# Attention's software pipeline one step shorter: probabilities turned 3 and values applied 4 steps behind the scores, the last logits in another order, expert-search columns 12 to 18 counted in one accumulation

## The chip, the cores and the metric

The kernel runs on one core of one Trainium2 chip. Its engines are TensorE (matmuls, PE in the profile, with its weight loads as PEld), VectorE (DVE), ScalarE (ACT), GpSimd (POOL) and SyncE (SP, which here only starts transfers). Each engine takes its own instructions in the order in which they were written and waits at an instruction until its inputs and its output buffer are free. The metric is device time in microseconds (us), the median of the runs.

## The reference

Three blocks follow one another: a sparse attention, a mixture of experts in which every token goes to one of 8 experts with room for 288 each, and a second mixture over 4 experts in which every token goes to all.

```python
scores = scale * np.matmul(q, k.transpose(0, 1, 3, 2))          # 4 batches, 8 heads, 576 x 64
mask_local = (rel >= 0) & (rel < stride)                        # heads 0..3, stride 32
mask_strided = (rel >= 0) & (pos[None, :] % stride == pos[:, None] % stride)   # heads 4..7
attn = softmax(where(masks, scores, -1e9)); attn_out = attn @ v
logits = x @ w_gate                                             # 2304 tokens, 8 experts
order = np.argsort(-logits.flatten())                           # best pairs first
for idx in order:
    tok, e = (int(idx) // E, int(idx) % E)
    if assigned[tok] >= 0 or counts[e] >= cap:
        continue
    assigned[tok] = e; counts[e] += 1
out[mask] = relu(x[mask] @ w1[e]) @ w2[e]                       # per expert
y = sum over 4 experts of p[:, e] * (relu(out @ v1[e]) @ v2[e])
```

## The kernel before

`front` computes the attention and the logits. The masks leave blocks only, so the work is cut into N = 40 units: for each of the 4 batches, 5 units of strided heads (`kind` 1, blocks of 126 or 108 rows) and 5 of local heads (128 queries by 96 keys, the last of them half as large). A loop over steps t writes out a software pipeline by hand. In step t stand, in this order of the program: dummy matmuls in the first 8 steps (`keep_busy`), then `tr_p(t-4)`, `norm(t-2)`, the queued pieces of token work (`late2`, `late`), up to two `piece`s (transposes of q and k of the next batch) around `exps(t-1)`, `logits(t-10)`, `av(t-5)` and `scores(t)`.

For one unit n: `scores` is TensorE's product of q and k into the PSUM tile `s`, which has one buffer, and VectorE's masked reduction into `sm` and `mx`. `exps` is ScalarE's exponential into `pr`, with row sums `su`. `norm` is VectorE's reciprocal `r` and a multiplication of `pr` by it on GpSimd. `tr_p` turns `pr` round on TensorE into the PSUM tile `pt`, which has one buffer, and ScalarE copies it out to `pT`. `av` multiplies by the values into the PSUM tile `av`, one buffer, and copies go into `hold`: by VectorE for strided units, by ScalarE for local ones. GpSimd also starts six transfers of v (`load_v`, line 78) in step 2, 12 and 22, ahead of that step's `norm`, and in step 28 one of `side` (line 403).

The copies of `piece` for q, and those of the logits, alternate between ScalarE and VectorE by a counter that all calls of `copy` raise:

```python
flip[0] += 1
ch = side_of[eng]
if ch == "a" or (ch == "f" and flip[0] % 2):
```

After the last scores (steps N = 40 to 45) the pipeline drains: `keep_busy(2)` puts two dummy matmuls of 512 columns into each of steps 41 to 44, the logits of units N-3 and N-1 (local groups 2 and 4 of the last batch) are made in steps 43 to 45, and `tokens` turns them to the layout `L`, tokens by 18 columns by 8 experts.

The search for the first expert begins with a count over these 18 columns: for each column `best` marks each token's best expert and `reach` compares its logit with 127 thresholds, and `first_count` multiplies the two on TensorE. Columns 0 to 11 are counted batch by batch during the attention, columns 12 to 13 in the drain, each group in its own PSUM accumulation that VectorE adds to `cnt`. Columns 14 to 17 follow in `search`, in `experts`, and are added to `cnt` there. `experts` begins with that search, in which TensorE and VectorE take turns, and with the transposes of the remaining attention rows (`deferred`, line 295 and 284); then rows are gathered by expert and the two mixtures run, which is the long rest of the kernel.

Of the kernel before, what the change touches and what calls it, by code (L numbers as in the profile page):

```python
# [18 lines left out]
FT = mybir.dt.float32  # L19
# [18 lines left out]
def front(tc, ident, hot, q, k, v, wg, dp, xd, L, ready, hold, deferred):  # L38
# [3 lines left out]
    with ExitStack() as st:  # L42
# [173 lines left out]
        def norm(n):  # L216
            T = U[n]
            rows, keys, na = shape(n)
            e = T["p"][:rows, :2 * na, :keys]
            r = wk.tile([128, 4], FT, name="r")[:rows, :2 * na]  # L220
            nc.vector.tensor_scalar(r, T["su"][:rows, :2 * na], 1e-9, None, op0=OP.add)
            nc.vector.reciprocal(r, r)
            nc.gpsimd.tensor_tensor(e, e, r[:, :, None].to_broadcast([rows, 2 * na, keys]), OP.mult)

        def tr_p(n):
            T = U[n]
# [89 lines left out]
                rows_q.pop(0)[1](*here, lambda o, i: copy(o, i, eng=eng))  # L316

        def logits(n):
            b, kind, g = units[n]
            if kind or g not in (2, 4):  # L320
                return
            i0, m = (0, 128) if g == 2 else (128, 160)
            p = LP[n] = ps.tile([128, 512], FT, name="xr", bufs=2)
            for h in range(4):
                nc.tensor.matmul(p[32 * h:32 * h + 32, :m], wgs[:, h], XTS[b].rearrange("p h j r -> p h (j r)")[:, h, i0:i0 + m], start=True, stop=False)
            if n < N - 1:
                logits_local(n)

        LP = {}

        def logits_local(n):
            b, kind, g = units[n]
            i0, m = (0, 128) if g == 2 else (128, 160)
            p = LP[n]
            for par in range(2):
                for hp in range(2):
                    c = 32 * (2 * par + hp)
                    nc.tensor.matmul(p[c:c + 32, :m], wgl[:, hp, 8 - 8 * par:40 - 8 * par], XTL[b][:, hp, 2 * i0 + par:2 * i0 + 2 * m:2],
                                     start=False, stop=True)
            lg = wk.tile([128, 160], FT, name="lg")  # L340
            copy(lg[:, :m], p[:, :m], eng="l")
            late.append(lambda: tokens(b, g // 4, lg))

        late, late2 = [], []
# [1 line left out]
        def tokens(b, q, lg):  # L346
            p = ps.tile([128, 512], FT, name="xr", bufs=2)
            nc.tensor.matmul(p[:, :16], lg[:, :128], four[:, :16], start=True, stop=True)
            copy(L[:, 4 * b + 2 * q:4 * b + 2 * q + 2, :], p[:, :16].rearrange("p (a e) -> p a e", a=2), eng="k")
            if q:  # L350
                w = slice(32 * b, 32 * b + 32)
                p = ps.tile([128, 512], FT, name="xr", bufs=2)
                nc.tensor.matmul(p[w, :16], lg[:, 128:], four[:, :16], start=True, stop=True)
                copy(L[w, 16:], p[w, :16].rearrange("p (a e) -> p a e", a=2), eng="k")
            if q == b // 3:
                return
            c0, c1 = (4 * b, 4 * b + 4) if q else (12, 14)
            late2.append(lambda: ready[0](c0, c1))
            late2.append(None)
            G = wk.tile([128, 4, 128], BF, name="g0")  # L360
            late2.append(lambda: ready[1](G, c0, c1))
            late2.append(None)
            late2.append(None)

            def count():
                p = ps.tile([128, 512], FT, name="xr", bufs=2)
                ready[2](G, p, c0, c1)
            late2.append(count)
# [13 lines left out]
        for t in range(N + 14):  # L382
            t_now[0] = t
            if t < N and t % 10 == 2 and units[t][0] + 1 < B:
                if units[t][0] + 2 < B:
                    load_qk(units[t][0] + 2, "s")
                load_v(units[t][0] + 1)
                if units[t][0] + 2 < B:
                    load_qk(units[t][0] + 2, "l")
                nxt = [(units[t][0] + 1, i) for i in ORDER]  # L390

            if t < N and t % 10 == 6 and units[t][0] + 1 < B:
                load_vl(units[t][0] + 1)
            if t == 28:
                side = cst.tile([128, 18, 8], FT, name="side")
                nc.gpsimd.memset(side, 0.0)
                nc.gpsimd.iota(side.bitcast(I32)[:, :, 4], pattern=[[1, 18]], base=0, channel_multiplier=18)
                rs = cst.tile([128, 18], FT, name="rs")
                nc.vector.tensor_reduce(rs, pr, AX.X, OP.add)
                nc.vector.tensor_scalar(rs, rs, 1e-9, None, op0=OP.add)  # L400
                nc.vector.reciprocal(rs, rs)
                nc.vector.tensor_tensor(side[:, :, :4], pr, rs[:, :, None].to_broadcast([128, 18, 4]), OP.mult)
                nc.gpsimd.dma_start(dap(xd, 512, [18 * XW, 128], [XW, 18], [1, 8]), side)
            if t % 10 == 6:
                todo += nxt
                nxt = []

            def at(d, f):
                if 0 <= t - d < N:
                    f(t - d)  # L410

            def pre():
                if todo and t:
                    piece(*todo.pop(0))

            def keep_busy(n):
                p = ps.tile([128, 512], FT, name="xr", bufs=2)
                for i in range(n):
                    nc.tensor.matmul(p, hot[:, :128], hot, start=True, stop=True)

            if BUSY[0] <= t < BUSY[1]:
                keep_busy(BUSY[2] + 2 * (t < 2))
            at(4, tr_p)
            if N < t < N + 5:
                keep_busy(2)
            at(2, norm)
            while late2:
                x = late2.pop(0)
                if x is None:
                    break  # L430
                x()
            while late:
                late.pop(0)()
            rows("o")
            pre()
            at(1, exps)
            rows("s")
            pre()
            if t < N:
                at(10, logits)  # L440
            elif t == N + 3:
                logits(N - 3)
            elif t == N + 4:
                logits(N - 1)
            elif t == N + 5:
                logits_local(N - 1)
            at(5, av)
            if t < N:
                scores(t)
        for x in late2 + late:  # L450
# [15 lines left out]
def route_consts(nc, cst):  # L466
# [56 lines left out]
                  cst.tile([128, NC, 8], FT, name="eq0")]  # L523
    nc.vector.memset(K["first"][2], 0.0)
    K["cnt"] = cst.tile([8, 128], FT, name="cnt0")
    K["sat"] = cst.tile([128, 1], BF, name="sat")
    nc.vector.memset(K["sat"], 0.0)
    return K
# [20 lines left out]
def first_best(nc, K, L, c0, c1):  # L549
    for _ in best(nc, K, L, K["first"], c0, c1):  # L550
        pass
# [6 lines left out]
def whole(oh, c):  # L558
    return oh[:, c:c + 4, :].rearrange("p a e -> p (a e)")


def first_count(nc, K, G, p, c0, c1):
    for c in range(c0, c1):
        nc.tensor.matmul(p[:, :127], whole(K["first"][2], c), G[:, c - c0, 1:128], start=c == c0, stop=c == c1 - 1)
    if c0 == 0:
        nc.vector.tensor_copy(K["cnt"][:, :127], p[:8, :127])
    elif c0 < 14:
        nc.vector.tensor_tensor(K["cnt"][:, :127], p[:8, :127], K["cnt"][:, :127], OP.add)


def search(nc, K, wk, ps, L, g, S, out):
# [5 lines left out]
    if g < 7:  # L577
# [5 lines left out]
        for r, (nb, sh) in enumerate(rounds):  # L583
# [6 lines left out]
            if g == 0 and r == 0:  # L590
                G = wk.tile([128, 4, 128], BF, name="G")
                first_best(nc, K, L, 14, 18)
                first_reach(nc, K, G, 14, 18)
                yield "2"
                first_count(nc, K, G, p, 14, 18)
                yield "p"
                nc.vector.tensor_tensor(junk[:, 1:], p[:8, :127], K["cnt"][:, :127], OP.add)
# [765 lines left out]
def attention_moe_moe(ctx, tc, q, k, v, wg, w1, w2, dp, v1, v2, out):  # L1363
    nc = tc.nc
    ctx.enter_context(tc.manual_schedule())
    cp = ctx.enter_context(tc.tile_pool(name="c", bufs=1))
    dr = ctx.enter_context(tc.tile_pool(name="dr", bufs=1, space=bass.MemoryType.DRAM))
    ident = cp.tile([128, 128], FT, name="ident")
    hot = cp.tile([128, 512], BF, name="hot")
    nc.vector.memset(hot, 1.0)  # L1370
    make_identity(nc, ident)
    L = cp.tile([128, 18, 8], FT, name="L")
    xd = dr.tile([2304, XW], FT, name="xd")
    side = dr.tile([2304, 8], FT, name="side")
    K = route_consts(nc, cp)
    yp = ctx.enter_context(tc.tile_pool(name="yp", bufs=1))
    ready = (lambda *a: first_best(nc, K, L, *a), lambda *a: first_reach(nc, K, *a), lambda *a: first_count(nc, K, *a))
    hold = lambda: yp.tile([128, 2304], FT, name="hold", bufs=3)
    deferred = []
    front(tc, ident, hot, q, k, v, wg, dp, xd, L, ready, hold, deferred)  # L1380
    experts(tc, ident, hot, K, L, xd, side, w1, w2, v1, v2, out, hold, deferred)
# [26 lines left out]
```

## Time and profile before

| | us |
|---|---|
| median of 3 runs | 1177.46 (1176.71 to 1178.22) |
| profiled execution, its own time | 1176.97 |
| its span, first to last instruction | 1175.3 |
| TensorE busy over the span | 1146.8 (98%) |
| exponentials of the last unit start | 107.26 |
| first instruction of the search on columns 14 to 17 | 117.49 |
| first matmul of the first expert | 146.09 |

Times in rows are counted from the span's start. The kernel has three stretches in time: the attention to about 108 us, the drain, the search and the gather to 146 us, and the experts from there to the end. Only the first two hold instructions that the change touches. "Step t" below is the step of the loop in which `scores(t)` is made, and "unit n" the unit.

### The profile page before, as it was taken

How to read it: one execution, taken by the hardware profiler on the slowest of the kernel's cores; microseconds unless marked ns; L12 is line 12 of the kernel's file. 1: busy time of each engine (PE TensorE's matmuls, PEld its weight loads, DVE VectorE, ACT ScalarE, POOL GpSimd, SP SyncE). 2: the span in 40 equal slices, each digit the busy share in tenths (PEclk: the TensorE clock that was granted, in tenths of full speed). 3: DMA queues.
4: the chain of work that ended last, by engine and by line, in shares of the span. 5: the costliest groups of instructions: out<-in, count | busy, mean ns of one | idle time of the engine just before them, and what ended most of it. 6: DMA issues, size and time to landing. Idle time of an engine off the chain costs nothing.

```text
span 1175.3 us, 24533 instructions
## 1 busy us (share of the span) xinstructions
PE 1146.8 (98%) x8845; PEld 1028.9 (88%) x8852; DVE 837.7 (71%) x2253; ACT 613.7 (52%) x1599; POOL 424.3 (36%) x474
## 2 busy tenths in 40 slices
PE   9999799999999999999999999999999999999997
PEld 6776598898998998999999999999898999899996
DVE  6787678787876787868665577776776776676663
ACT  6997455451442433555544555555555555555552
POOL 6453120001010100001105465556756666656652
PEclk9999899999999999999999999999999999999999
DMA  7871665553351543656565333333433333333320
GB/s 176 179 186 32 178 214 164 171 156 93 109 172 57 178 121 91 209 176 208 167 201 176 96 108 99 100 108 93 141 91 108 107 92 108 127 108 104 94 73 36
DMA packets 203372, 152.96 MB, mean 130 GB/s; under 512 B 42569, under 2 KB 169871, under 8 KB 202963
## 3 DMA queue, kind: packets, MB, share of 16 engines
q1 hardware_dynamic: 198930, 140.91, 40.8%
q0 software_dynamic: 4320, 10.49, 2.8%
q8 instruction: 69, 1.13, 0.4%
q14 instruction: 53, 0.43, 0.1%
HBM read 141.77 MB, written 9.58 MB: 129 GB/s over the span
## 4 chain that ended last, share of the span: by engine, by line
PE 85%; ACT 4%; POOL 3%; DVE 3%; issue 3%; DMA 2%; POOLq 0%; SPq 0%; DVEq 0%; ACTq 0%
PE o L994 38%; PE h L994 19%; PE h L1226 9%; PE pa L1226 7%; PE pb L1226 3%; ACT pr L213 2%; DMA raw<-in_moe_w_dram 1%; POOL wl L1213 1%; PE pa L620 1%; PE pt L230 1%; POOL out_dram L1090 1%; DVE wl L769 1%; PE s L194 1%; PE av L250 1%; ACT pT L139 1%
## 5 line engine op out<-in xcount | busy, mean ns | idle before, releaser
L769 DVE TENSOR_TENSOR wl<-raw,wh 128x512 fp32r<-128x512 f32 x352 | 268.6, 792 | 4.6 <-DMA raw<-in_moe_w_dram 1.0
L887 ACT ACTIVATE hh<-h 128x256 fp32r<-128x256 f32 (+1 forms) x256 | 99.9, 390 | 271.5 <-PE h L994 192.8
L994 PE MATMUL o<-wh,hh 128*128 128x512 f32 x576 | 226.8, 394 | 1.0 <-DVE hold L769 0.5
L994 PE MATMUL o<-wl,hh 128*128 128x512 f32 x576 | 226.5, 393 | 0.0
L994 PE MATMUL o<-wh,hl 128*128 128x512 f32 x576 | 226.0, 392 | 0.0
L1213 POOL TENSOR_TENSOR wl<-raw,wh 128x512 fp32r<-128x512 f32 x96 | 122.0, 1292 | 197.3 <-ACT wh L1212 165.5
L769 DVE SCALAR_TENSOR_TENSOR hl<-h,hh 128x256 fp32r<-128x256 f32 (+1 forms) x256 | 109.8, 429 | 116.9 <-ACT hh L887 112.4
L867 ACT CAST wh<-raw 128x512 fp32r<-128x512 f32 x272 | 159.9, 619 | 61.3 <-DMA raw<-in_moe_w_dram 59.3
L914 POOL DMA_INDIRECT xg<-xd,idx x24 | 27.7, 1154 | 332.2 <-DVE idx L769 196.1
L994 PEld LDWEIGHTS o<-wh,hl 128*128 128x128 f32 x576 | 108.3, 188 | 23.1
L994 PEld LDWEIGHTS o<-wh,hh 128*128 128x128 f32 x576 | 108.3, 188 | 7.2 <-PE h L994 0.7
L994 PEld LDWEIGHTS o<-wl,hh 128*128 128x128 f32 x576 | 108.4, 188 | 5.7
L769 DVE TENSOR_TENSOR wl<-sums,wh 128x512 fp32r<-128x512 f32 x96 | 82.0, 855 | 28.5 <-ACT wh L1199 28.4
L1199 ACT CAST wh<-sums 128x512 fp32r<-128x512 f32 x96 | 59.7, 623 | 80.0 <-POOL sums L1187 57.2
L994 PE MATMUL h<-xh,wh 128*128 128x288 f32 x256 | 76.3, 298 | 1.3 <-DVE hl L769 1.0
L994 PE MATMUL o<-hh,wl 128*128 128x288 f32 x256 | 76.8, 300 | 0.0
L994 PE MATMUL o<-hh,wh 128*128 128x288 f32 x256 | 76.7, 300 | 0.0
L994 PE MATMUL h<-xh,wl 128*128 128x288 f32 x256 | 75.9, 296 | 0.6 <-DVE wl L769 0.6
L994 PE MATMUL o<-hl,wh 128*128 128x288 f32 x256 | 76.1, 297 | 0.0
L994 PE MATMUL h<-xl,wh 128*128 128x288 f32 x256 | 76.0, 297 | 0.1
L994 PE MATMUL h<-y256h,wl 128*128 128x256 f32 x256 | 73.5, 287 | 0.0
L994 PE MATMUL h<-y256l,wh 128*128 128x256 f32 x256 | 73.2, 286 | 0.0
(318 smaller groups left out, 2919.5 us busy)
## 6 DMA issues: line engine op xcount, KB each, us to landing
raw<-in_moe_w_dram SPq DMA_DIRECT2D x464, 256.0 KB
vl<-in_v_dram SPq DMA_DIRECT2D x16, 192.0 KB
ql<-in_q_dram SPq DMA_DIRECT2D x12, 144.0 KB
kl<-in_k_dram SPq DMA_DIRECT2D x12, 144.0 KB
qs<-in_q_dram SPq DMA_DIRECT2D x2, 576.0 KB
ks<-in_k_dram SPq DMA_DIRECT2D x2, 576.0 KB
xd<-y SPq DMA_DIRECT2D x2, 576.0 KB
xd<-hl SPq DMA_DIRECT2D x5, 192.0 KB
```

What stands on the lines that cost most here:

```text
L139: nc.scalar.copy(out, in_)
L194: nc.tensor.matmul(out[:rows], lt, rt, start=True, stop=True)
L213: nc.scalar.activation(e[:rows, j, :keys], T["s"][:rows, j, :keys], AF.Exp, scale=-1.0, bias=T["mx"][:rows, j:j + 1], accum_out=T["su"][:r ...
L230: nc.tensor.transpose(p[:keys, rows * j:rows * j + rows], T["p"][:rows, j, :keys], ident[:rows, :rows])
L769: return f(*args, **kw)
L867: nc.scalar.copy(c["h"][:, sl], c["raw"][a])
L887: nc.scalar.activation(hi, src, AF.Relu)
L914: nc.gpsimd.indirect_dma_start(out=xg[:, k, :], out_offset=None, in_=xd, in_offset=bass.IndirectOffsetOnAxis(ap=idx[:, k:k + 1], axis=0))
L994: nc.tensor.matmul(out, a, b, start=start, stop=stop)
L1199: nc.scalar.copy(S["W"][nm][0], src[nm]())
L1213: nc.gpsimd.tensor_tensor(l, r, h.bitcast(FT), OP.subtract)
L1226: mmx = lambda o, a, b, first, lastm, n: (nc.tensor.matmul(o, a, b, start=first, stop=lastm, skip_group_check=True), tick(n / 2315 + 0.009))
```

## The change

`tr_p` stands 3 and `av` 4 steps behind the scores, where they stood 4 and 5 behind. Within a step `tr_p` moves from the front to a place after the pieces and `exps`. In the drain the dummy matmuls stay in step N+1 alone, in another PSUM tile (`tr`), and the logits of units N-3 and N-1 are cut into a strided and a local half and placed one or two steps earlier. The last unit's `norm` multiplication goes to VectorE and its logits' copy to ScalarE. For columns 12 and 13, `best` and `reach` run directly after one another and write to a tile of their own, `g12`; their count moves into `search`, into the same PSUM accumulation as columns 14 to 17.

```diff
-            nc.gpsimd.tensor_tensor(e, e, r[:, :, None].to_broadcast([rows, 2 * na, keys]), OP.mult)
+            (nc.vector if n == N - 1 else nc.gpsimd).tensor_tensor(e, e, r[:, :, None].to_broadcast([rows, 2 * na, keys]), OP.mult)
...
         def logits(n):
+            if not units[n][1] and units[n][2] in (2, 4):
+                logits_strided(n)
+                logits_local(n)
+
+        def logits_strided(n):
             b, kind, g = units[n]
-            if kind or g not in (2, 4):
-                return
...
-            if n < N - 1:
-                logits_local(n)
...
-            copy(lg[:, :m], p[:, :m], eng="l")
+            copy(lg[:, :m], p[:, :m], eng="y" if n == N - 1 else "l")
...
             c0, c1 = (4 * b, 4 * b + 4) if q else (12, 14)
+            if not q:
+                late2.extend((lambda: ready[0](c0, c1), lambda: ready[1](ready[3], c0, c1)))
+                return
...
-                p = ps.tile([128, 512], FT, name="xr", bufs=2)
+                p = ps.tile([128, 512], FT, name="xr" if t < N else "tr", bufs=2)
...
-            at(4, tr_p)
-            if N < t < N + 5:
-                keep_busy(2)
             at(2, norm)
...
+            if t == N + 1:
+                keep_busy(2)
+            if t == N + 2:
+                logits_strided(N - 3)
+            at(3, tr_p)
             if t < N:
                 at(10, logits)
+            elif t == N + 2:
+                logits_local(N - 3)
             elif t == N + 3:
-                logits(N - 3)
+                logits_strided(N - 1)
             elif t == N + 4:
-                logits(N - 1)
-            elif t == N + 5:
                 logits_local(N - 1)
-            at(5, av)
+            at(4, av)
...
-        nc.tensor.matmul(p[:, :127], whole(K["first"][2], c), G[:, c - c0, 1:128], start=c == c0, stop=c == c1 - 1)
+        nc.tensor.matmul(p[:, :127], whole(K["first"][2], c), G[:, c - c0, 1:128], start=c == c0 and c0 < 14, stop=c == c1 - 1 and c0 != 12)
...
-    elif c0 < 14:
+    elif c0 < 12:
...
                 yield "2"
+                first_count(nc, K, K["g12"], p, 12, 14)
                 first_count(nc, K, G, p, 14, 18)
```

TensorE in steps 22 and 23, before. Rows name the output tile and the inputs: `tr` rows are pieces (`ql`, `kl`), `pt` rows are `tr_p`, `av` rows are `av`, `s` rows are `scores`; the first row is `tr_p` of unit 18, the fifth that of unit 19, and the last, which already belongs to step 24, that of unit 20:

```order
L230 MATMUL pt<-ident,pr 96x128 x4
L169 MATMUL tr<-ident,ql 128x96 x6
L250 MATMUL av<-pT,vl 64x64 x8
L194 MATMUL s<-kS,qS 108x108 x4
L230 MATMUL pt<-ident,pr 96x128 x2
L169 MATMUL tr<-ident,kl 128x96 x6
L250 MATMUL av<-pT,vl 64x64 x8
L194 MATMUL s<-kS,qS 108x108 x4
L230 MATMUL pt<-ident,pr 126x126 x4
```

The same two steps in the changed kernel:

```order
L169 MATMUL tr<-ident,ql 128x96 x6
L230 MATMUL pt<-ident,pr 96x128 x2
L250 MATMUL av<-pT,vl 64x64 x8
L194 MATMUL s<-kS,qS 108x108 x4
L169 MATMUL tr<-ident,kl 128x96 x6
L230 MATMUL pt<-ident,pr 126x126 x4
L250 MATMUL av<-pT,vl 64x64 x4
L194 MATMUL s<-kS,qS 108x108 x4
```

In each step the `pt` row has moved from the front to behind the piece, and it is that of the next unit: unit 20's (126x126) now stands in step 23, ahead of unit 19's `av` and of the scores of unit 23.

TensorE in the drain, before: from `tr_p` of the last unit (96x128 x2) in step 43 on. `hot` rows are the dummies, `wgs` and `wgl` rows the strided and local logits, and the `av` row is that of unit 38:

```order
L230 MATMUL pt<-ident,pr 96x128 x2
L419 LDWEIGHTS hot
L419 MATMUL xr<-hot 128x512
L419 LDWEIGHTS hot
L419 MATMUL xr<-hot 128x512
L325 MATMUL xr<-hold,wgs 32x128 x4
L338 MATMUL xr<-hold,wgl 32x128 x4
L250 MATMUL av<-pT,vl 64x64 x8
L419 LDWEIGHTS hot
L419 MATMUL xr<-hot 128x512
L419 LDWEIGHTS hot
L419 MATMUL xr<-hot 128x512
```

The same in the changed kernel, from `tr_p` of unit 38 in step 41 on; the `four` row is `tokens` of unit 37, and the last `av` row that of the last unit:

```order
L230 MATMUL pt<-ident,pr 96x128 x4
L250 MATMUL av<-pT,vl 64x64 x8
L328 MATMUL xr<-hold,wgs 32x128 x4
L230 MATMUL pt<-ident,pr 96x128 x2
L339 MATMUL xr<-hold,wgl 32x128 x4
L250 MATMUL av<-pT,vl 64x64 x8
L349 MATMUL xr<-four,lg 128x16
L328 MATMUL xr<-hold,wgs 32x160 x4
L250 MATMUL av<-pT,vl 64x64 x4
```

The dummies are gone from here, the last unit's transpose stands between two halves of the logits, and `tokens` and the strided half of the last logits come ahead of the last `av`.

ScalarE while the first batch's local units are at work (from `exps` of unit 4 on), before. `pr,su` rows are `exps`, `qS` and `kS` rows copies of pieces:

```order
L213 ACTIVATE pr,su<-sm,mx 128x96 x4
L139 COPY kS<-tr 128x4x4x18
L139 COPY pT<-pt 108x432
L213 ACTIVATE pr,su<-sm,mx 128x96 x4
L139 COPY kS<-tr 128x4x4x18
L139 COPY pT<-pt 108x432
L213 ACTIVATE pr,su<-sm,mx 128x96 x4
```

And in the changed kernel:

```order
L139 COPY pT<-pt 108x432
L141 ACTIVATE qS<-tr 128x4x4x18
L213 ACTIVATE pr,su<-sm,mx 128x96 x4
L139 COPY kS<-tr 128x4x4x18
L139 COPY pT<-pt 108x432
L141 ACTIVATE qS<-tr 128x4x4x18
L213 ACTIVATE pr,su<-sm,mx 128x96 x4
L139 COPY kS<-tr 128x4x4x18
```

By the alternating counter the `qS` copies of this batch now fall to ScalarE. Over the kernel ScalarE has 12 `qS` copies where it had 8, 9 `qL` where it had 7, and 5 of `L` (128x16) where it had 4; VectorE has as many fewer. GpSimd's order is the same but for the last `norm`.

## Rows read from the trace of the kernel before

**Rows 1.** Busy time by engine, 62 to 86 us: start:end, length, PE, PEld, DVE, ACT, POOL, clock, DMA share, GB/s

```profile
62.00:86.00 24.00, 23.13 (x360) 18.44 (x358) 20.54 (x134) 22.07 (x103) 14.03 (x21) 1.00 0.84 191
```

**Rows 2.** Waits of ScalarE, 20 to 107 us: total us, times, longest us

```profile
ACT pT L139 <- PE pt L230: 4.9, 11, 0.8
```

**Rows 3.** Groups of ScalarE, 20 to 107 us: count, then busy us and mean ns

```profile
L141 ACT ACTIVATE qS<-tr 128x288 f32<-128x288 f32 x4 | 1.7, 434 | 0.0
```

**Rows 4.** Timeline around step 36: start us, length us, engine, line, operation

```profile
98.52 0.58 PE L230 MATMUL pt<-ident,pr 108*108 108x108 f32 x4
...
99.02 0.65 PE L243 MATMUL av<-pT,vs 126*64 126x126 f32 x8
...
99.61 0.56 PE L197 MATMUL s<-kL,qL 64*64 64x96 f32 x16
...
99.64 0.39 ACT L213 ACTIVATE pr<-sm,mx 128x96 f32<-128x96 f32 x1
...
100.23 0.26 DVE L204 CUSTOM_DVE_ANT_0 sm<-s,lm 128x96 f32<-128x96 f32 x1
...
100.61 0.42 PE L325 MATMUL xr<-hold,wgs 128*32 128x128 f32 x8
...
101.09 0.51 ACT L139 COPY pT<-pt 108x432 f32<-108x432 f32 x1
...
101.19 0.59 PE L243 MATMUL av<-pT,vs 108*64 108x108 f32 x8
...
101.49 0.39 ACT L213 ACTIVATE pr<-sm,mx 128x96 f32<-128x96 f32 x1
```

**Rows 5.** Timeline, steps 20 to 24: VectorE, GpSimd, TensorE

```profile
63.53 0.28 DVE L204 CUSTOM_DVE_ANT_0 sm<-s,bd 126x126 f32<-126x126 f32 x1
...
65.24 3.69 POOL L78 DMA_DIRECT2D vs<-in_v_dram  x6 [0.37 <-PE s L194]
...
68.90 1.07 POOL L223 TENSOR_TENSOR pr<-pr,r 126x504 f32<-126x504 f32 x1
...
70.03 0.65 PE L230 MATMUL pt<-ident,pr 126*126 126x126 f32 x4
...
71.75 0.44 PE L194 MATMUL s<-kS,qS 64*108 64x108 f32 x4 [0.45 <-DVE mx L204]
```

**Rows 6.** Timeline, steps 12, 13, 28, 29: GpSimd and TensorE

```profile
43.59 2.05 POOL L223 TENSOR_TENSOR pr<-pr,r 126x504 f32<-126x504 f32 x2
...
44.48 0.63 PE L194 MATMUL s<-kS,qS 64*108 64x108 f32 x8
...
82.94 1.68 POOL L223 TENSOR_TENSOR pr<-pr,r 128x384 f32<-128x384 f32 x2
...
83.93 0.40 PE L197 MATMUL s<-kL,qL 64*64 64x96 f32 x8
```

**Rows 7.** Timeline after the last scores: ScalarE, TensorE, VectorE

```profile
107.26 0.38 ACT L213 ACTIVATE pr<-sm,mx 128x96 f32<-128x96 f32 x1
...
109.09 0.64 PE L230 MATMUL pt<-ident,pr 128*96 128x128 f32 x4
...
110.71 0.42 PE L230 MATMUL pt<-ident,pr 128*96 128x128 f32 x2
...
114.01 0.48 PE L325 MATMUL xr<-hold,wgs 128*32 128x160 f32 x8 [0.26 <-ACT L L139]
...
117.28 0.28 DVE L568 TENSOR_TENSOR cnt<-xr,cnt 8x127 f32<-8x127 f32 x1 [0.52 <-PE xr L564]
...
117.49 0.16 DVE L769 TENSOR_REDUCE m<-L 128x4 f32<-128x32 f32 x1
```

**Rows 8.** Two counts in the timeline, and busy time with granted clock between

```profile
113.13 0.39 PE L564 MATMUL xr<-g,oh 128*128 128x127 bf16 x4
...
118.80:122.20 3.40, 2.92 (x17) 2.55 (x17) 2.23 (x10) 2.01 (x6) 0.00 (x0) 0.50 0.41 116
...
119.28 0.58 PE L564 MATMUL pa<-G,oh 128*128 128x127 bf16 x4 [0.59 <-DVE G L769]
```

More of the change, by code (lines that the diff above doesn't have):

```diff
@@ L525, in route_consts @@
     K["cnt"] = cst.tile([8, 128], FT, name="cnt0")
+    K["g12"] = cst.tile([128, 2, 128], BF, name="g12")
     K["sat"] = cst.tile([128, 1], BF, name="sat")
@@ L1376, in attention_moe_moe @@
     yp = ctx.enter_context(tc.tile_pool(name="yp", bufs=1))
-    ready = (lambda *a: first_best(nc, K, L, *a), lambda *a: first_reach(nc, K, *a), lambda *a: first_count(nc, K, *a))
+    ready = (lambda *a: first_best(nc, K, L, *a), lambda *a: first_reach(nc, K, *a), lambda *a: first_count(nc, K, *a), K["g12"])
     hold = lambda: yp.tile([128, 2304], FT, name="hold", bufs=3)
```

## The prediction

> **What bounds the kernel now.** I read the table of windows first, for the middle of the attention: TensorE is busy 96% and ScalarE 92% of the stretch from 62 to 86 us, VectorE 86% (20.54 of 24), GpSimd 58% [rows 1]. Two engines are close to full, and each takes its work in order. The waits of ScalarE then tell which of them leads where: between 20 and 107 us ScalarE stood 11 times before the copy of `pT` until TensorE had made `pt`, 4.9 us together [rows 2]. In most of these steps TensorE is the later one. In steps 34 to 39 no pieces are left and ScalarE leads: in the timeline of step 36 its exponentials begin at 99.64 and those of the next unit at 101.49, 1.85 us later, 1.45 of it for the exponentials (to the copy at 101.09) and 0.40 for that copy's place [rows 4].
>
> After the last scores there is a chain of latencies and no full engine: from the last exponentials (107.26) to the first instruction of the search on the last four columns (117.49) 10.23 us pass, and the steps in it follow the transposes by 1.62 us (109.09 to 110.71) [rows 7]. What comes behind, search, gather and experts, needs all columns counted, so I let it shift 1:1 with the end of the drain. The question is therefore how much later the last exponentials begin, and how much shorter the drain becomes. Times are summed against the profiled execution's own 1176.97 us; the median is 0.49 above it. Plus is later. A measurement of this kernel tells about 0.2%, 2.35 us, from no change.
>
> **1. More work ahead of the last scores: +1.1.** With distances one shorter, TensorE has by the last scores made one more unit's transpose and one more unit's values. The transpose takes 0.50 (98.52 to 99.02) and the values 0.59 (99.02 to 99.61) [rows 4]. If TensorE leads, both count (1.1); if ScalarE does, they fill holes (0). I take 1.1, since the waits of rows 2 say that TensorE leads.
>
> **2. The transpose comes closer behind GpSimd's `norm`: +3.5.** `norm(n)` stands in step n+2. Its reader stood first in step n+4 and now stands at the end of step n+3. GpSimd's own order does not change, and in three places it is late because it starts transfers of v first, or has two `norm` in a row.
>
> Step 23: six transfers take 3.69 us from 65.24, so `norm(20)` runs from 68.90 to 69.97; `tr_p(20)` starts at 70.03 and `scores(24)` at 71.75, after 0.45 of waiting for VectorE [rows 5]. Now `tr_p(20)` stands ahead of `av(19)` and `scores(23)`. From 69.97: 0.1 for the handover (0.06 there, rounded up), 0.5 transpose, 0.3 for half a unit of values, 0.6 scores, 0.3 of the next piece that is not yet done, 0.5 `tr_p(21)`, 0.6 values; that puts `scores(24)` at 72.9, 1.1 later. (Durations of TensorE are pitches as in rows 4; the 0.3 of the piece is an estimate.)
>
> Step 13: two `norm` take 2.05 from 43.59, so the first ends at about 44.65, and `scores(13)` stood at 44.48 [rows 6]. Now they stand behind `tr_p(10)`: 44.65 + 0.1 + 0.5 + 0.3 = 45.55, 1.1 later. Step 29: the first of two ends at about 83.8, and `scores(29)` stood at 83.93 [rows 6]. Now 83.8 + 0.1 + 0.5, then the logits that stand between, 0.58 (100.61 to 101.19) [rows 4], and values 0.6: 85.6, 1.7 later, of which I keep 1.3, because the following steps have slack on TensorE while ScalarE leads. Sum 3.5. It is 0 if these delays are made up by the steps behind them, and 3.9 if none is.
>
> **3. ScalarE's waits for `pt` go: -1.0.** A transpose late in its step is one of a unit that was normalised long before the copy needs it, so the 4.9 us of rows 2 have no cause left. Where TensorE leads, this gives nothing; where ScalarE leads, it gives all. Bounds 0 and -3.4 (some 70% of it; the rest lies in the steps that part 2 delays). I take -1.0, near the first.
>
> **4. Steps without pieces: +1.5.** The old period there is 1.85. The new order makes a cycle over two steps: a transpose, then values, then scores, 1.09 (98.52 to 99.61); scores to the first masked reduction 0.62 (99.61 to 100.23); that reduction and its handover 0.40 (0.26 and an estimated 0.14); four exponentials 1.45; the copy's place 0.40 [rows 4]; a handover of 0.1, after which the next transpose but one may write. That is 4.06 for two steps, 2.03 for one, 0.18 more than now, in five steps 0.9. In steps 37 and 39 the logits now stand inside the cycle; 0.58 each would be 1.2 for both, of which I count half, 0.6. Bounds 0 (if buffers free earlier than so) and 2.0.
>
> **5. The drain: -2.3.** One round of the chain fewer, 1.62 (109.09 to 110.71); the wait of the last strided logits for a copy, 0.26; the addition of columns 12 and 13 to `cnt`, 0.28, with its place ahead of the search, together 0.4 [rows 7]. So 10.23 becomes 7.95. The added matmuls in the search's accumulation need no PSUM buffer or addition of their own; they lie before the count of columns 14 to 17, while VectorE still makes its `G`, and I count them at nothing (without that cover half of a count of four, 0.2 to 0.3 by rows 8). Bounds -3.4 (two rounds) and -1.5 (the round alone).
>
> **6. Costed at nothing.** Six more copies of q on ScalarE (four `qS`, two `qL`) at 434 ns a copy [rows 3] are 2.6 us of ScalarE; VectorE loses as much. They lie beside TensorE's 96%; where ScalarE leads they cost up to all of it. The last `norm` on VectorE and the last logits' copy on ScalarE save a change of engine, but the transpose of the last unit waits for the copy of the one before it anyway. Six of eight dummies fewer: TensorE's clock. A count of four matmuls took 0.39 in the drain and 0.58 in the search, and from 118.80 to 122.20 the granted clock was 0.50, the lower of its two levels, after TensorE and VectorE had begun to take turns [rows 8]. If the lower level comes into the drain, its 2.3 us of TensorE pieces (an estimate from the rows above) become 2.3 x 0.58/0.39 = 3.4, 1.1 more. I take nothing: transposes and logits now fill part of where the dummies were.
>
> The Trainium skill ("TensorE: Matmul & The Clock Gate", section "HAM oscillation — how this bites in real kernels") says that a TensorE which waits between short bursts is put back to half clock and begins the next burst cold; the clock of 0.50 in the search agrees with it. By that rule taking dummies out of a chain of waits costs, and the sum would get the 1.1.
>
> **Sum.** 1.1 + 3.5 - 1.0 + 1.5 - 2.3 = +2.8: 1179.8 by the profiled execution, 1180.3 as a median.
>
> **The rivals.** *ScalarE leads everywhere and the change wins.* TensorE's 96% is made of matmuls whose ends are modelled, its weight loads fill only 77% [rows 1]. Then part 1 costs nothing, of part 2 only the 1.3 of step 29 stays, part 3 gives its 3.4, part 4 costs 1.5 and part 5 gives 2.3: -2.9, a median of 1174.6. It decides where the 4.9 us of rows 2 delay the exponentials behind them by more than 2 us. Against it speak the same waits: an engine that waits 11 times for TensorE is not the later one there.
>
> [...]
>
> *Gains and stalls cancel.* The delays of part 2 are half made up behind them (1.75), part 1 is half hidden (0.5), part 4 costs 0.9 without logits, part 3 gives 1.0, part 5 gives 2.3: -0.1, a median of 1177.4. For it speaks that buffers let engines drift by a step; against it that `s`, `pt` and `av` have one buffer each.
>
> *Heavier.* The copies on ScalarE cost half (1.3) and the drain runs at the lower clock (1.1): +5.2, a median of 1182.7. For it: 92% of ScalarE [rows 1]; against it: copies in steps where it waits.
>
> **How the numbers follow.** Forecast (1178.5 to 1182) 0.45; ScalarE leads 0.24; cancelled 0.20; heavier 0.11. Faster by over 2.35 us is the second case, 0.24. Of the forecast's case I count 0.13 within 2.35 of before, since its value is only 0.5 beyond: same 0.33, slower 0.32 + 0.11 = 0.43. The range goes from the faster rival's 1174.6 to half a us beyond the heavy one's, 1183.2; 0.12 is below, 0.05 above. The forecast's own range is 1178.5 to 1182.
>
> **What would show it.** In the changed profile `tr_p(20)`, and `tr_p(10)` and `tr_p(26)`, wait for GpSimd's `pr`; a start of theirs without that wait makes part 2 wrong. ScalarE's waits for `pt` shrink to under 2 us. The last exponentials begin at about 112 us (107.26 + 1.1 + 3.5 - 1.0 + 1.5 = 112.4); before 108, ScalarE led and the forecast is wrong. From there to the search's first maximum 8.0 us, not 10.2; over 9.5 would make part 5 wrong. A granted clock under 0.8 in those 8 us shows the heavier rival. Behind the search the stretches keep their lengths; if the first expert's matmuls do not move with the end of the drain, 1:1 is wrong.

## The result and the profile after

The changed kernel takes 1187.47 us (1185.96 to 1187.88), the kernel before 1177.7 on the same chip: a ratio of 1.0085, interval 1.0073 to 1.0098, about 10 us slower. The profiled execution has a span of 1186.2, 10.9 above that of before.

Groups in the timeline of the changed kernel, TensorE and GpSimd in steps 12 and 13, beside [rows 6] (start, length, engine, line, operation, wait before it):

```profile
41.58 3.69 POOL L78 DMA_DIRECT2D vs<-in_v_dram  x6 [0.37 <-PE s L194]
...
43.36 0.63 PE L194 MATMUL s<-kS,qS 64*108 64x108 f32 x8
...
45.26 2.04 POOL L223 TENSOR_TENSOR pr<-pr,r 126x504 f32<-126x504 f32 x2
...
46.38 1.10 PE L230 MATMUL pt<-ident,pr 126*126 126x126 f32 x4 [1.12 <-POOL pr L223]
...
48.04 1.06 PE L194 MATMUL s<-kS,qS 64*108 64x108 f32 x8
```

`tr_p(10)` waits for GpSimd's `norm(10)`, as forecast. What was not forecast: the transpose takes 1.10 and the scores 1.06, where the scores of the step before took 0.63. The windows over the same stretch and over steps 23 and 29 (start:end, length, busy time of TensorE, its weight loads, VectorE, ScalarE and GpSimd with the number of instructions, granted clock, DMA share, GB/s):

```profile
44.00:46.00 2.00, 1.06 (x8) 0.69 (x8) 1.93 (x12) 2.00 (x12) 2.00 (x4) 1.00 0.56 141
46.00:48.00 2.00, 1.62 (x12) 1.21 (x12) 0.66 (x2) 1.20 (x6) 1.30 (x2) 0.57 0.88 201
48.00:50.00 2.00, 2.00 (x15) 1.74 (x14) 0.86 (x9) 0.90 (x5) 0.00 (x0) 0.50 0.83 175
50.00:52.00 2.00, 2.00 (x15) 1.35 (x13) 0.56 (x3) 1.83 (x8) 0.91 (x1) 0.50 0.98 218
52.00:54.00 2.00, 2.00 (x20) 1.66 (x22) 1.52 (x12) 0.60 (x3) 0.00 (x0) 0.72 0.97 211
54.00:56.00 2.00, 1.97 (x36) 1.44 (x32) 1.97 (x16) 2.00 (x11) 1.15 (x2) 1.00 1.34 226
...
74.00:76.00 2.00, 1.04 (x14) 0.81 (x14) 1.83 (x4) 1.46 (x8) 1.58 (x2) 1.00 0.99 265
76.00:78.00 2.00, 2.00 (x26) 1.56 (x28) 1.32 (x12) 1.48 (x7) 0.44 (x2) 1.00 1.06 233
...
90.00:92.00 2.00, 1.40 (x12) 0.96 (x16) 0.23 (x1) 1.27 (x7) 1.32 (x2) 0.66 0.93 109
92.00:94.00 2.00, 2.00 (x36) 1.32 (x32) 0.33 (x1) 0.34 (x1) 0.00 (x0) 0.50 0.01 1
```

After a wait of 1.12 us the granted clock fell to 0.50, the lower of TensorE's two levels (1.2 GHz in place of 2.4), and was back at 1.00 some 7 us later. The "full" 2.00 of busy time at 48 us is 15 matmuls, against 36 (not all of the same size) at 54 us: busy share alone hides it. The waits from 20 to 118 us (total, times, longest):

```profile
PE pt L230 <- POOL pr L223: 3.6, 3, 1.3
...
PE pt L230 <- ACT pT L139: 2.9, 6, 0.7
ACT pT L139 <- PE pt L230: 2.1, 3, 0.8
```

The three waits for `pr` are those of `tr_p(10)`, `tr_p(20)` and `tr_p(26)`, the latter two in the timeline at 74.96 and 90.60:

```profile
74.96 0.65 PE L230 MATMUL pt<-ident,pr 126*126 126x126 f32 x4 [1.26 <-POOL pr L223]
...
90.60 1.07 PE L230 MATMUL pt<-ident,pr 128*96 128x128 f32 x4 [1.24 <-POOL pr L223]
```

In the first of these the clock stayed at 1.00 (windows from 74, transposes 0.65), in the second it fell (windows from 90, transposes 1.07). ScalarE's waits for `pt` fell from 4.9 [rows 2] to 2.1. In the drain, beside [rows 7]:

```profile
118.92 0.38 ACT L213 ACTIVATE pr<-sm,mx 128x96 f32<-128x96 f32 x1
...
122.04 0.42 PE L230 MATMUL pt<-ident,pr 128*96 128x128 f32 x2
...
123.70 0.48 PE L328 MATMUL xr<-hold,wgs 128*32 128x160 f32 x8
...
126.64 0.19 DVE L777 TENSOR_REDUCE m<-L 128x4 f32<-128x32 f32 x1
```

From the last exponentials to the search 7.72 us in place of 10.23, and windows over it show the clock at 1.00:

```profile
119.00:126.60 7.60, 6.81 (x109) 4.69 (x110) 4.64 (x21) 4.25 (x18) 0.86 (x2) 1.00 0.02 4
```

So the 10.9 us are: last exponentials 11.66 later (118.92 - 107.26), drain 2.51 shorter, everything behind 1.75 longer. Where the 11.66 arise, the starts of the scores tell. The table gives the offset, that is, how many us they start behind those of the kernel before, by step, in the profiled execution of the changed kernel and of the experiments below (e1 to e6 and e9 to e11). The first column is how late an execution began its first steps; costs are read along a row.

| scores of step | 2 | 5 | 12 | 16 | 22 | 25 | 28 | 30 | 33 | 39 |
|---|---|---|---|---|---|---|---|---|---|---|
| changed | 0.07 | 1.33 | 1.48 | 5.23 | 5.15 | 6.62 | 6.81 | 10.08 | 10.25 | 12.43 |
| e1 | -0.14 | 1.12 | 1.27 | 1.38 | 1.46 | 1.64 | 1.82 | 4.02 | 4.19 | 6.37 |
| e2 | 0.23 | 1.49 | 1.63 | 3.09 | 3.22 | 4.84 | 5.02 | 7.17 | 7.33 | 9.52 |
| e3 | 0.29 | 1.54 | 1.02 | 3.47 | 4.21 | 6.53 | 6.58 | 10.80 | 11.47 | 13.66 |
| e4 | 0.53 | 1.78 | 1.94 | 3.10 | 3.24 | 6.91 | 7.10 | 8.91 | 9.07 | 10.45 |
| e5 | 0.36 | 1.62 | 1.78 | 1.88 | 1.96 | 2.13 | 2.32 | 2.95 | 3.12 | 5.30 |
| e6 | 0.71 | 1.97 | 1.22 | 0.80 | 1.70 | 1.86 | 1.74 | 2.18 | 2.35 | 3.73 |
| e9 | 0.09 | 0.45 | 0.52 | 0.10 | 1.02 | 1.19 | 1.08 | 1.52 | 1.69 | 3.08 |
| e10 | 0.63 | -0.14 | -0.85 | -0.85 | -0.85 | -0.85 | -0.85 | -0.85 | -0.85 | -0.84 |
| e11 | 0.53 | 0.89 | 0.51 | 0.11 | 1.02 | 1.18 | 1.06 | 1.51 | 1.68 | 1.35 |

In the changed kernel the steps of this row are 1.26 (start), 3.75, 1.47 and 3.27 (the three late norms), 2.18 (steps without pieces), and 0.43 elsewhere.

### The profile page after: what moved, and what is told of

Its sections match the earlier page's. It is cut to its first block, busy times and chain, and to the rows that moved or that the text cites. A ratio compares the mean times of both kernels' runs of the same rounds, so it can differ in the third digit from the quotient of the medians.

```text
span 1186.2 us, 24520 instructions
## 1 busy us (share of the span) xinstructions
PE 1149.0 (97%) x8840; PEld 1027.5 (87%) x8846; DVE 834.6 (70%) x2245; ACT 616.2 (52%) x1607; POOL 424.9 (36%) x473
## 4 chain that ended last, share of the span: by engine, by line
PE 85%; POOL 3%; issue 3%; DVE 3%; DMA 3%; ACT 2%; POOLq 0%; SPq 0%; DVEq 0%; ACTq 0%
PE o L1002 38%; PE h L1002 19%; PE h L1234 9%; PE pa L1234 7%; PE pb L1234 3%; DMA raw<-in_moe_w_dram 2%; PE pt L230 1%; POOL wl L1221 1%; PE pa L628 1%; ACT pr L213 1%; POOL out_dram L1098 1%; PE s L194 1%; PE av L243 1%; PE av L250 1%; PE tr L158 1%
```

## The experiments

Theory A: late norms make TensorE wait, and the waits bring the lower clock. Theory B: the extra work ahead of the last scores and ScalarE's added copies are the cost. Each ratio is against the kernel before, run beside the experiment on the same chip: its median was 1178.16 with e1 to e4, 1176.54 with e5 to e8 and 1176.5 with e9 to e11. The changed kernel's ratio is 1.0085.

**e1: GpSimd's transfers to SyncE.**

```diff
-(nc.gpsimd if b and t > 4 else nc.sync).dma_start(T["vs"] ...
+nc.sync.dma_start(T["vs"] ...
...
-nc.gpsimd.dma_start(dap(xd, 512, ...
+nc.sync.dma_start(dap(xd, 512, ...
```

> The changed kernel with GpSimd's transfers of v and of side started by SyncE, so that its norm(10), norm(20) and norm(26) no longer stand behind them. Theory A (late norms make TensorE wait, and the waits bring its lower clock): the three waits of 1.1 to 1.3 us for pr go, the granted clock stays at 1.00 from 44 to 56 and from 90 to 94 us, and the time falls by 6 to 8 us, from 1187.5 to about 1180. Theory B (the extra work ahead of the last scores and the q copies on ScalarE are what costs): the last exponentials move by less than 1.5 us and the time stays at 1186 to 1188. If only the transfers and not the pairs of norms matter, step 29 keeps a wait of 0.5 or more.

Measured 1182.23, ratio 1.0047 (1.0028 to 1.0066). As theory A said, no wait of `pt` for `pr` is left, the granted clock stays at 1.00 in the windows over the three places, and steps 12 to 28 cost 0.55 in place of 5.3. The time fell by less than it said (some 4.5 us by the ratios, not 6 to 8): with more transfers on SyncE `vl` came late to step 29, where the offset grew by 2.20 (TensorE's matmuls waited 1.0 for `vl`; what the rest is, is not shown). Waits from 20 to 112 us and windows of e1:

```profile
PE av L250 <- DMA vl<-in_v_dram: 1.0, 3, 0.4
...
44.00:54.00 10.00, 9.39 (x127) 7.01 (x125) 8.48 (x61) 9.78 (x45) 3.98 (x5) 1.00 0.50 118
70.00:80.00 10.00, 9.30 (x138) 6.84 (x138) 7.13 (x55) 9.77 (x46) 4.70 (x6) 1.00 0.52 124
84.00:94.00 10.00, 8.44 (x121) 6.50 (x121) 5.18 (x33) 7.64 (x33) 2.44 (x5) 1.00 0.50 115
```

**e2: dummies in the waits.**

```diff
+            if t in (13, 23, 29):
+                p = ps.tile([128, 512], FT, name="pt")
+                for _ in range(6):
+                    nc.tensor.matmul(p, hot[:, :128], hot, start=True, stop=True)
             at(3, tr_p)
```

> The changed kernel with six dummy matmuls of 512 columns (about 0.22 us each) ahead of the transposes of steps 13, 23 and 29, where TensorE waits 1.1 to 1.3 us for GpSimd. The waits stay, only TensorE is not idle in them. Theory A: the clock stays at 1.00 after steps 13 and 29, and the part of the loss that is clock, estimated at 2.7 us there (3.8 from the scores of step 12 to 15 less the wait of 1.1) and 2.0 (3.3 less 1.2), comes back: about 1183. Theory B, or a lower clock that costs nothing because ScalarE leads: 1187 to 1189, the dummies being added work.

Measured 1184.63, ratio 1.0060 (1.0038 to 1.0081). Timeline and windows of e2:

```profile
45.26 1.46 PE L447 MATMUL pt<-hot 128*128 128x512 bf16 x6
...
45.42 2.05 POOL L223 TENSOR_TENSOR pr<-pr,r 126x504 f32<-126x504 f32 x2
...
46.87 0.62 PE L230 MATMUL pt<-ident,pr 126*126 126x126 f32 x4
...
46.00:48.00 2.00, 1.85 (x20) 1.03 (x20) 0.80 (x3) 1.34 (x7) 1.46 (x2) 1.00 1.03 216
48.00:50.00 2.00, 2.00 (x26) 1.56 (x24) 1.42 (x11) 1.48 (x9) 0.21 (x1) 1.00 1.06 185
...
90.00:92.00 2.00, 2.00 (x46) 1.49 (x38) 0.83 (x6) 0.94 (x4) 0.00 (x0) 1.00 0.97 178
```

`norm(10)` is as late as in the changed kernel and the transpose still starts at its end, but the clock stays at 1.00 and the transpose takes 0.62. By the ratios the time fell by some 3 us although 18 matmuls were added (the two intervals overlap a little). It stayed above theory A's 1183: the three places cost 1.46, 1.62 and 2.15 in the table, 0.8 more in all than the waits alone cost below. Of e2's four executions three took 1183.06 to 1184.95, at a mean granted clock of 0.994 to 0.996, and one took 1188.16 at 0.991; the trace is of one of the three, so it is not shown that the dummies hold the clock every time.

**e3: q copies on the engines of before.**

```diff
+            if eng == "q":
+                ch = QPIN.pop(0)
```

> The changed kernel with each copy of q on the engine that it had before (ScalarE 8 qS and 7 qL in place of 12 and 9). Theory A: less than 1 us, 1186.5 to 1188, waits and clock in steps 13 and 29 unchanged. Theory B: 2 to 4 us back, 1183.5 to 1185.5, with the stretches between the three late steps shorter.

Measured 1191.28, ratio 1.0106 (1.0079 to 1.0133), above the expectations of both theories. The clock fell after all three waits in its profile:

```profile
48.00:50.00 2.00, 2.00 (x12) 1.65 (x12) 1.30 (x11) 1.75 (x10) 0.81 (x1) 0.50 1.06 210
76.00:78.00 2.00, 2.00 (x18) 1.49 (x18) 1.27 (x11) 1.11 (x6) 0.17 (x1) 0.56 1.25 262
94.00:96.00 2.00, 2.00 (x12) 1.71 (x12) 0.73 (x4) 1.46 (x6) 0.83 (x1) 0.50 0.00 0
```

Its time says nothing on the copies; ahead of the first fall they gave 0.7 (from step 5 to 12 the offset fell by 0.52 where the changed kernel's rose by 0.15).

**e4: a second place for `pt`.**

```diff
+            if n > 30 and n % 2:
+                p = ps.tile([128, 512], FT, name="tr", bufs=2)
...
```

> The changed kernel with the transposes of odd units from 31 on in the tile of the pieces (tr), so that two units of pt can stand at once in the steps without pieces. If the cycle transpose, values, scores, exponentials, copy of pT sets the pace there (2.03 us a step), the scores of units 33 to 39 come at about 1.85 us a step and the time falls by 1.5 to 2.3 us, to about 1185.5. If the pace is set by something else (one tile for scores or for av), nothing changes, 1187 to 1188.

Measured 1186.12, ratio 1.0075 (1.0058 to 1.0091). Steps 33 to 39 cost 1.38 in place of 2.18, so the second place takes 0.8 of it away. Up to step 33 its program is that of the changed kernel, and yet in this execution the clock stayed at 1.00 after step 13 and fell at step 23:

```profile
48.00:50.00 2.00, 2.00 (x26) 1.56 (x24) 1.42 (x11) 1.47 (x9) 0.20 (x1) 1.00 0.86 179
74.00:76.00 2.00, 2.00 (x21) 1.62 (x21) 0.19 (x1) 0.84 (x2) 0.43 (x1) 0.50 1.32 187
76.00:78.00 2.00, 2.00 (x15) 1.46 (x13) 1.08 (x11) 1.82 (x9) 0.88 (x1) 0.50 1.31 232
```

**e5: the transfers one a step behind `norm`.**

```diff
-                    (nc.gpsimd if b and t > 4 else nc.sync).dma_start( ...
...
+                    if b > 1 and t > 4:
+                        vq.append(go)
...
             at(2, norm)
+            if vq:
+                vq.pop(0)(nc.gpsimd)
+            if t == N:
+                sq.pop()()
```

> The changed kernel with GpSimd's transfers of v for the last two batches started one a step behind its norm (steps 12 to 17 and 22 to 27), and the transfer of side in step 40. GpSimd still starts them, but no norm stands behind six at once, and SyncE is not longer than in the changed kernel. Theory A: TensorE's three waits for pr (3.6 us together) go, none for vl takes their place in step 29, the clock stays at 1.00 to the drain; the last exponentials begin 3 to 4.5 us later than before (107.26), the time is 1178 to 1180.5. If it comes out below 1176, the shorter pipeline gains by itself and only the norms spoil it; if it stays above 1182, something else than the late norms costs there.

Measured 1179.92, ratio 1.0027 (1.0016 to 1.0038): 6.8 us of the 10 are gone (0.58% of 1177). `norm(10)` runs ahead of its transpose, the last exponentials are 4.53 late, and the clock stays at 1.00 in the windows over the three late places:

```profile
43.25 1.02 POOL L229 TENSOR_TENSOR pr<-pr,r 126x504 f32<-126x504 f32 x1 [1.75 <-DVE r L228]
...
45.41 0.62 PE L236 MATMUL pt<-ident,pr 126*126 126x126 f32 x4
...
111.79 0.38 ACT L219 ACTIVATE pr<-sm,mx 128x96 f32<-128x96 f32 x1
...
119.51 0.19 DVE L787 TENSOR_REDUCE m<-L 128x4 f32<-128x32 f32 x1
...
44.00:54.00 10.00, 9.42 (x130) 7.05 (x127) 8.27 (x55) 9.79 (x47) 6.50 (x10) 1.00 1.04 194
70.00:80.00 10.00, 9.26 (x128) 6.83 (x131) 7.63 (x59) 9.78 (x46) 7.48 (x12) 1.00 1.09 230
84.00:94.00 10.00, 9.28 (x136) 7.25 (x137) 6.74 (x48) 8.55 (x38) 2.93 (x5) 1.00 0.52 103
```

**e6: e5 with the edits of e3 and e4.**

> e5 with the copies of q on the engines that they had before, and the second place for pt from unit 31 on. Without clock falls the two should show their own size: the q copies 0.4 to 0.9 us (the scores of step 11 came 0.46 earlier with them than in the changed kernel), the second pt 0.8 (the scores of steps 33 to 39 spread by 1.4 us more than before, in place of 2.2). Together 1.2 to 1.7 below e5, about 1177.5 to 1179. If ScalarE leads, more: 1175 to 1177.

Measured 1176.3, ratio 0.9997 (0.9989 to 1.0006), no difference from before. The last exponentials are at 110.22 and the search at 117.94, 1.57 earlier than in e5 (1.93 counted from the scores of step 2, since this execution began 0.35 later). That is the size expected of the two edits; the total lies lower than expected, because the span is 3.1 shorter than e5's and the other 1.5 arise behind the search. What this version still loses up to the last exponentials, 2.96 (110.22 - 107.26), its shorter drain (7.72 in place of 10.23) gives back but for 0.45.

**e7: the kernel before with e5's transfers** (`side` in step 41).

> A control: the kernel before with the same transfers of v spread over steps, and side's transfer in step 41. Its transposes stand two steps behind norm, so theory A says it gains next to nothing: at most the wait of 0.45 in step 24, 1177.5 to 1178.2 on this chip's scale. If GpSimd's transfers cost by themselves (not by the place of the transposes), it gains 2 us or more.

Measured 1176.08, ratio 0.9998 (0.9989 to 1.0007): with two steps between `norm` and transpose, spreading the transfers gains nothing that can be measured.

**e8: the drain's edits alone, on the kernel before** (the hunks of the diff for the last `norm`, the last `lg` copy, `g12`, `first_count` and the dummies' tile).

> The kernel before, pipeline distances and order of the loop unchanged, with those edits of the drain that need no shorter pipeline: columns 12 and 13 counted in the search's accumulation, best and reach in one go, the dummies in the tile of the pieces, the last norm on VectorE, the last logits' copy on ScalarE. If one round less is what shortened the drain (1.62 of 2.3), these give 0.4 to 0.9: 1177.0 to 1177.6. If they are the larger part, 1.5 to 2.3: about 1176.

Measured 1176.67, ratio 0.9997 (0.9988 to 1.0007). Its drain lasts 9.61 (timeline of e8):

```profile
107.06 0.38 ACT L213 ACTIVATE pr<-sm,mx 128x96 f32<-128x96 f32 x1
...
116.66 0.19 DVE L774 TENSOR_REDUCE m<-L 128x4 f32<-128x32 f32 x1 [0.19 <-ACT L L139]
```

The edits give 0.62 of the 2.51. The rest, 1.89, is left for the round less, the logits placed with it and the six dummies fewer, which no run separates. The search began 0.83 earlier than before, and the total did not fall.

**e9 and e10: no dummies in steps 4 to 7**, in e6 and in the kernel before.

```diff
-BUSY = (0, 8, 2)
+BUSY = (0, 4, 2)
```

> e6 without the two dummy matmuls in each of steps 4 to 7 (8 dummies, 0.22 us from one to the next). In the traces the extra unit's transpose and values stand in steps 3 and 4 as 1.3 us that no later step made up. If TensorE leads from there to step 28 (the reading by which that work counts in full), taking 1.8 us of TensorE out there brings the last exponentials 1.3 to 1.8 earlier: 1174.5 to 1175.2, or 1.0 to 1.8 below before. If another engine leads there, nothing: as before. If the clock falls in those steps, 2 or more slower.

> The control: the kernel before without the same eight dummies. If TensorE leads there too, 1.3 to 1.8 us faster than before, as much as e9 below e6, and the shorter pipeline has no share in it. If the longer pipeline has nothing else to fill steps 4 and 5 with, its clock falls or the gain is smaller, 0 to 0.8.

Measured 1177.38, ratio 1.0006 (0.9996 to 1.0015), and 1177.06, ratio 1.0010 (1.0001 to 1.0019). Counted from the scores of step 2, the last exponentials of e10 came 1.47 earlier than before (106.42 - 17.39 against 107.26 - 16.76): between steps 4 and 12 of the kernel before TensorE leads, by the larger part of the 1.8. Those of e9 came as in e6 (109.57 - 16.85 = 92.72 and 110.22 - 17.47 = 92.75): of 0.89 gained by step 5, 0.07 was left by step 11. In the shorter pipeline of e6 TensorE does not lead there; which engine does, these runs do not show. Neither total fell: the search of e10 began at 116.65, 0.84 earlier than before, and nothing of it reached the end.

**e11: e9 with late scores first.**

```diff
             at(3, tr_p)
+            if 33 < t < N:
+                scores(t)
...
-            if t < N:
+            if t < 34:
                 scores(t)
```

> e9 with the scores of units 34 to 39 ahead of the logits and of the values in their steps, right behind the transpose. If the way from the transpose over values and logits to the scores sets the pace of the steps without pieces, the scores of steps 34 to 39 spread no more than before and the time falls another 1.0 to 1.5 us. If ScalarE's work alone sets it, or the values then come late, nothing: as e9.

Measured 1176.48, ratio 1.0001 (0.9992 to 1.0010). The scores of step 39 came 1.73 earlier than in e9, but the last exponentials only 0.31 (109.26): with the scores out of the way ScalarE sets the pace, as in [rows 4]; between the exponentials of unit 33 and those of unit 39 it stands idle for only 0.76 of 12.66 us. No version beats the kernel before.

## Why the prediction was wrong, point by point

The sign was right and the size was not: +2.8 forecast, about +10 measured, outside the range. The step that failed is part 2, in two ways: it priced the three waits at 3.5 and put TensorE's clock after them at nothing, where the waits took 4.4 and the clock another 4.1. Of the 8.1 us by which the measured 10.9 (spans) exceed the forecast 2.8, the clock is 4.05, the waits 0.94, the stretch behind the search 1.75 and the steps without pieces 0.68; the last 0.7 is spread over the other terms. Of the signs that were named, the waits at the three transposes and the drain (7.72, for 8.0) came as forecast, ScalarE's waits almost (2.1, for under 2); the last exponentials, at 118.92 in place of 112.4, did not.

*Part 2's price left out the clock.* The mechanism is shown: the waits stand at the three transposes named, and without them (e5) 6.8 us go. The waits by themselves cost 1.16 (step 12 to 16 in e4), 1.47 (22 to 25 in the changed kernel) and 1.81 (28 to 30 in e4), each in an execution in which the clock did not fall there: 4.4 in place of 3.5. A fall adds, at the same three places, 3.75 - 1.16 = 2.6, 3.67 - 1.47 = 2.2 and 3.27 - 1.81 = 1.5. The changed kernel's profile has two of them, the first and the third, 4.1 us. I had weighed the clock, in part 6 and in the heavier rival, but only where dummies were taken out; in the drain it stayed at 1.00. Step 29, of whose 1.7 I had kept 1.3 for slack behind it, took 1.81: there was no slack.

*Part 2's delays were reckoned from GpSimd's old times.* I let the first `norm` of step 13 end at 44.65. It began at 45.26, since GpSimd's transfers stand behind its own `norm(9)` (at 38.94 before, at 40.60 now) and so had moved 1.67 later with the pipeline (from 39.91 in the timeline of before to 41.58). A delay in front moves the engine that causes the next one too. By the old times the 1.1 of part 1 would have been part of the delay at step 13, and adding both would have counted it twice; that the sum is right there (1.16 on top of an offset of 1.48) is luck, because GpSimd had moved.

*Part 1* was mis-sized by little: 1.26 for 1.1, in steps 2 to 5 (1.25 to 1.26 in e1 to e6 too). That it stays for good is so with the changed kernel's copies of q (e5: 1.42 from step 2 to 12); with those of before (e6) 0.51 is left by step 12. So the copies on ScalarE have a share in holding it there; it is not TensorE alone that does so, as I had read from [rows 2].

*Part 3* gave a little less than its 1.0, and not where I had it: ScalarE's waits shrank by 2.8, and the offset did not fall between the late places (+0.43 in all). The last exponentials follow their scores by 0.83 (118.92 - 118.09) instead of 1.60 (107.26 - 105.66); these 0.77 are all that came back.

*Part 4*: 2.18 for 1.5. The cycle over `pt` is 0.8 of it (e4, e6). The remainder I had put down to the logits inside the cycle, and e11, whose scores stand ahead of logits and values, took it out of the scores. The last exponentials gained only 0.3 by that, so most of it is not the logits: e11 still takes 12.66 from the exponentials of unit 33 to those of unit 39, where the kernel before takes 11.60.

*Part 5*: 2.51 for 2.3, and by e8 the edits that need no shorter pipeline are the smaller part of it, 0.62.

*Part 6*: the copies of q on ScalarE were costed at nothing and cost about 1.1: from step 5 to 33, ahead of the second place for `pt`, e5 lost 1.50 and e6, with the copies where they were, 0.38.

*The shift behind the search is not 1:1.* From the search to the end before took 1057.8 (1175.3 - 117.49), the changed kernel 1059.6, and all thirteen profiled executions 1057.1 to 1060.7. Up to the first expert the shift still holds (its first matmul comes at 155.03, 8.94 later than before, the search 9.15 later). In the changed kernel 1.3 arises near 230 us, where ScalarE waits 3.58 for weights:

```profile
229.56 1.30 ACT L875 CAST wh<-raw 128x512 fp32r<-128x512 f32 x2 [3.58 <-DMA raw<-in_moe_w_dram]
```

The same wait in the kernel before:

```profile
218.96 1.24 ACT L867 CAST wh<-raw 128x512 fp32r<-128x512 f32 x2 [2.19 <-DMA raw<-in_moe_w_dram]
```

What sets the length of these waits stays open, and with it why gains of 0.8 ahead of the search (e8, e10) vanish.

Of the rivals, ScalarE leading everywhere is refuted: with the late norms gone (e5) the kernel is still slower, and in steps 4 to 12 of the kernel before TensorE leads (e10). That gains and stalls cancel is refuted by the table: no delay is made up in the steps behind it (5.23 to 5.15, 6.62 to 6.81). Of the heavier rival the copies came true (1.1 for 1.3) and the clock in the drain did not. Theory B holds for what e5 leaves, as far as the traces reach: e6 takes 1.57 us of it out ahead of the search, and the other 1.5 of the 3.1 between their spans lies in the stretch behind it that no run explains.

## What to carry to other kernels

When a stage is moved closer to its producer, price each wait that it uncovers twice: the wait, and TensorE at 1.2 GHz for the microseconds after it; here two falls cost 4.1 and the three waits 4.4. Move the producer's own schedule along with the delays before reading how late it is, and look at what else its engine starts in that step: issuing them one a step, behind `norm`, was worth 6.8 us here and nothing in the kernel before.

## What the runs showed of the hardware

The fall of the clock after a wait is not certain. In the changed kernel, e3 and e4 TensorE waited nine times 1.1 us or more for `pr`, and the granted clock fell after six of them, at different places in executions of the same instructions. With dummies in the three waits it fell after none in the traced execution of e2, and e1, e5 and e6, which do not have the waits, kept 1.00 there. Nor has a fall one price: in e3 the clock was back at 1.00 by 52 us after the first wait and by 78 us after the second, and these places cost 2.45 and 2.32 in the table, while the third, longer at 0.50, cost 4.22. What decides whether it falls, and for how long, stays open.

By the Trainium skill ("TensorE: Matmul & The Clock Gate", section "HAM oscillation — how this bites in real kernels") a TensorE that waits for its inputs between bursts starts the next one at half clock. These runs agree after six of the nine waits in the attention, where I had not looked for it, and not after the other three; in the drain the clock stayed at 1.00, with TensorE busy for 6.81 of 7.60 us.
